# Moving a third token tile's projections from the attention loop into the entry of the linear-attention stage

## The chip, the cores and the metric

The kernel runs on one core of one Trainium2 chip. The metric is device time in microseconds (us) of one execution. The profiled execution gives the trace from which everything below is read; its span starts at its first instruction.

## The reference

Four residual blocks on a sequence of 2048 tokens of width 576, with 32 heads of 18: attention with one shared key/value head (A), then linear attention with Hedgehog features (B), then both again with the same weights.

```python
def A(x, wq, wk, wv, wo):            # one key/value head for 32 query heads
    q = heads(x @ wq); k = x @ wk; v = x @ wv
    p = softmax(einsum("bhqd,bkd->bhqk", q, k) * Dh ** -0.5)
    return merge(einsum("bhqk,bkd->bhqd", p, v)) @ wo
def B(x, wqkv, w_phi, wo):
    q, k, v = split_heads(x @ wqkv)
    phi = lambda t: concat([softmax(t @ w_phi), softmax(-(t @ w_phi))])   # per head
    kv, z = einsum("bhsf,bhsd->bhfd", phi(k), v), phi(k).sum(s)
    return merge(einsum("bhqf,bhfd->bhqd", phi(q), kv) / (phi(q) @ z + 1e-6)) @ wo
for block in (A, B, A, B): x = x + block(layernorm(x))
```

## The kernel before, in words

**Stages.** Tokens are held as 16 tiles of 128. A layer is an A and a B. Per layer there is an attention loop (`attend`) and then a stage that reads the linear attention out and prepares the next layer's queries (in the second layer: writes the output).

**The loop.** 32 groups (16 query tiles by two halves of the heads) run over 16 key tiles and two halves: 1024 units a layer. A unit is two score matmuls on TensorE (PE, L518), one exp of 128x1024 on ScalarE (ACT, L994), and its share of the values matmuls (L806). Results are normalised on VectorE (DVE, L908 to L916), split in high and low parts, and written to DRAM. When both groups of a tile are there, they are read back as `on`.

**What is slipped in.** PE has time beside ACT's exps, and a generator (`stream`, from L1238 on) hands out pieces of other work, a PSUM bank at a time ("fillings", 14 matmuls of 128x288 each, L240): the output projection of a finished tile (weights `wd`, two fillings) and `mix` of a token tile whose residual is done (six fillings: keys `wa`, values `wb`, queries `wc`). In `mix`, `feature_start` (L551 to L558) makes the feature exponents of a half of the heads, `feature_end` (L563 to L565) divides by their sums, `update_state` (L595, 64 small matmuls) adds keys times values to the state `kv` (L601), and the finished query features are turned in blocks of 32 (L647) and spilled to DRAM as `phi`. In the loop DVE does all this; in the stage the products of L565 are on GpSimd (POOL), and features are flipped by PE (L621). In the first layer `fold_phi` (L309 to L364) also runs in the loop: it multiplies `w_phi` into the query and key weights, ten slabs of 288 KB that ACT's queue loads (L332).

**What sets the order.** The order of PE and DVE in the loop is the order in which the code writes the instructions (`in_order` chains them). In the stage a scheduler places them by dependence and priority.

**The entry of the stage.** Tiles 14 and 15 can't be mixed in the loop. `last_mix` (L690) mixes tile 14 beside `last_group` (L858), which normalises the last group: copy of the accumulators (L861), transposes (L864), reciprocals (L868), widening (L870), transposes back (L873), product (L874), split (L133, L134), eight writes and six reads of `on` (L838, L851 to L856). Then come the output projection of tile 15, tile 15's own tokens (`xo`, `xsc`) and mix, the state's transposes (L740), `kvt` (L741), the block matrix `kvb`, and the read-out (L757) and its projection, tile by tile. `prepare` loads `wob` and, in the first layer, `wq` beside it.

Of the kernel before, what the change touches and what calls it, by code (L numbers as in the profile page):

```python
# [61 lines left out]
def kernel(ctx, tc, x_in, wq, wk, wv, wo, wqkv, w_phi, wob, out):  # L62
# [246 lines left out]
    def fold_phi(ps, tmp):  # L309
# [16 lines left out]
        def fetch(n):  # L326
# [3 lines left out]
            st = stage.tile([P, D], F32, name="fstage")  # L330
# [9 lines left out]
        st, following = fetch(0), fetch(1)  # L340
# [3 lines left out]
        short(pl, st)  # L344
        yield -110
        for n, (half, k) in enumerate(units):
            later = fetch(n + 2)
# [15 lines left out]
            short(pl, following)  # L363
            nc.sync.dma_start(scratch[half, k * P : (k + 1) * P, :], fo[:, :D])  # L364
            st, following = following, later
# [240 lines left out]
    def queries(xs, e, st, ps, copies):  # L606
# [3 lines left out]
        if copies is A:  # L610
            for b in range(2):
                feature_end(e, b, G)

# [63 lines left out]
    def mix(i, xs, st, ps, spill, loads, slow, after):  # L677
# [5 lines left out]
        for b in range(2):  # L683
            feature_end(eq, b, V)
        blocks = bw.tile([P, NKG, P], F32, name="pht").rearrange("p a b -> p (a b)")
        spilling = block_transpose(blocks[:, : 2 * D], eq.rearrange("p h s d -> p (h s d)"), spill[i], SPILL)
        next(spilling)
        slow.append(spilling)

    def last_mix(i, stats, st, pool, ps, spill):  # L690
        xn = layer_norm(i, stats, pool, A, "xn" if pool is bw else "xo")
        yield STAGE
        xs = pool.tile([P, 9, P], F32R, name="xs" if pool is bw else "xs3")
        yield from transposed(xn, xs, ps, A, LOE)
        yield STAGE
        if pool is bw:
            ek, eq = (bw.tile([P, H, 2, DH], F32, name=tag) for tag in ("featk", "featq"))
        else:
            both = pool.tile([P, 9, PW], F32, name="xsc").rearrange("p a b -> p (a b)")
            ek, eq = (both[:, k * 2 * D : (k + 1) * 2 * D].rearrange("p (h s d) -> p h s d", s=2, d=DH)  # L700
                      for k in range(2))
        vb = yield from keys_values(i, xs, ek, st, ps, A)
        if pool is bw:
            yield from queries(xs, eq, st, ps, A)
        yield STAGE
        yield from update_state(ek, vb, st, ps)
        st["mixed"] += 1
        yield STAGE
        if pool is not bw:
            yield from queries(xs, eq, st, ps, A)  # L710
            yield STAGE
            yield STAGE
        pht = st["sp"].tile([P, NKG, P], F32, name="phs", bufs=1)
# [14 lines left out]
    def finish_state(st, sp, ps):  # L728
        while st["mixed"] < len(st["left"]):
            yield STAGE  # L730
# [417 lines left out]
    with first, tc.tile_pool(name="ps0", bufs=7, space=PSUM) as ps:  # L1148
# [8 lines left out]
        def advance(job):  # L1157
            while next(job) is not STAGE:
                pass
# [319 lines left out]
```

## Time and profile before

| | us |
|---|---|
| three runs | 2711.14, 2717.02, 2718.07 |
| median | 2717.02 |
| profiled execution | 2717.63 |
| its span | 2715.9 |
| PE busy | 2609.6 (96%) |
| ACT busy | 2149.7 (79%) |
| DVE busy | 1258.2 (46%) |
| first loop, from its first scores | 126.0 to 1248.0 |
| first layer's stage, to its first read-out projection | 1248.0 to 1301.5 |
| second loop's last values end | 2565.0 |
| second stage, to its first read-out projection | 2565.0 to 2618.7 |

A row of the timeline has start and duration, engine, line, operation, output and inputs, how many are merged, and in brackets the idle time of the engine ahead of it with what ended it. A row of windows has the stretch and its length, then busy time (and count) of PE, PE's weight loads, DVE, ACT and POOL, the granted clock of PE as a share of full speed, the DMA engines' busy share and their GB/s.

### The profile page before, as it was taken

To read this page: it belongs to the slowest core of one execution; us is meant where nothing else is said; L and a number is where in the kernel's file an instruction comes from. 1 tells how busy PE (TensorE), PEld (TensorE's weight loads), DVE (VectorE), ACT (ScalarE), POOL (GpSimd) and SP (SyncE) were. 2 spreads that over 40 slices of the span, in tenths; PEclk is the share of its full clock that TensorE was granted. 3 is DMA by queue.
4 is the path that set the end of the run, shared out by engine and by line. 5 is a ranking of instruction groups with operands and counts; after the bars stand their busy time and mean duration, and the time that the engine had idled before them with its cause. 6 is when DMAs were issued, how large, how long until landed. Compare 5 with 4: busy or idle time off the path is not lost. (4 is left out here: it accounts for less than half of the span.)

```text
span 2715.9 us, 55458 instructions
## 1 busy us (share of the span) xinstructions
PE 2609.6 (96%) x22030; PEld 1454.6 (54%) x22030; DVE 1258.2 (46%) x2867; ACT 2149.7 (79%) x2511; POOL 56.8 (2%) x98
## 2 busy tenths in 40 slices
PE   7989999999999999999998999999999999999989
PEld 6633345554555544456997244444444444444588
DVE  8532244445454444445775124444444444444455
ACT  4588898998889879995334999999999999999711
POOL 1000000000000000001000000000000000000010
PEclk9999999999999999999999999999999999999989
DMA  6554134222223212214755412222222222221164
GB/s 192 169 186 140 50 111 130 69 66 58 53 67 72 59 46 57 57 47 112 233 155 161 144 51 59 59 59 59 59 59 59 59 59 59 57 59 48 40 190 144
DMA packets 476349, 245.05 MB, mean 90 GB/s; under 512 B 222706, under 2 KB 433842, under 8 KB 476082
## 3 DMA queue, kind: packets, MB, share of 16 engines
q1 hardware_dynamic: 474610, 238.46, 31.8%
q8 instruction: 177, 2.90, 0.5%
q10 hardware_dynamic: 1472, 2.95, 0.3%
q14 instruction: 90, 0.74, 0.1%
HBM read 133.86 MB, written 105.51 MB: 88 GB/s over the span
## 5 line engine op out<-in xcount | busy, mean ns | idle before, releaser
L994 ACT ACTIVATE pt<-sc 128x1024 f32<-128x1024 f32 x2036 | 1925.4, 1047 | 211.2 <-PE sc L518 191.1
L518 PE MATMUL sc<-qst,kst 56*128 56x512 f32 x3840 | 687.1, 449 | 23.5 <-ACT pt L994 23.0
L518 PEld LDWEIGHTS sc<-qst,kst 56*128 56x128 f32 x3840 | 317.2, 184 | 534.3 <-ACT pt L994 479.4
L806 PE MATMUL acc<-pt,vst 128*32 128x512 f32 x4096 | 499.0, 600 | 0.6 <-DVE featk L551 0.2
L806 PE MATMUL ps<-pt,vst 128*32 128x512 f32 x4048 | 483.5, 601 | 6.5 <-DVE featk L551 6.1
L806 PEld LDWEIGHTS ps<-pt,vst 128*32 128x32 f32 x4048 | 110.1, 109 | 237.4 <-issue 224.2
L806 PEld LDWEIGHTS acc<-pt,vst 128*32 128x32 f32 x4096 | 106.0, 109 | 218.4 <-issue 212.1
L240 PE MATMUL ps<-wahi,xs 128*128 128x288 f32 x792 | 174.5, 306 | 5.7 <-DVE featk L551 3.4
L304 DVE TENSOR_TENSOR xc<-xc,acc 128x288 f32<-128x288 f32 x60 | 27.2, 453 | 321.1 <-PE acc L240 321.1
L240 PEld LDWEIGHTS ps<-wahi,xs 128*128 128x128 f32 x792 | 131.6, 191 | 14.1 <-DVE featk L551 4.2
L240 PE MATMUL ps<-walo,xs 128*128 128x288 f32 x440 | 130.1, 298 | 0.0
L240 PE MATMUL acc<-wdhi,on 128*128 128x288 f32 x540 | 119.7, 307 | 2.0 <-DMA on<-od 2.0
L240 PE MATMUL ps<-wchi,xs 128*128 128x288 f32 x495 | 111.2, 310 | 0.0
L131 ACT ACTIVATE xs<-ps 128x512 fp32r<-128x512 f32 x36 | 21.4, 595 | 112.6 <-PE ps L290 106.3
L396 PE MATMUL ps<-xsc,wbhi 128*128 128x256 f32 x576 | 107.6, 286 | 0.7 <-ACT xsc L131 0.7
L551 DVE COPY featq<-ps 128x288 f32<-128x288 f32 x47 | 21.5, 458 | 179.7 <-PE ps L240 179.6
L418 ACT ACTIVATE pc<-ps 128x256 fp32r<-128x256 f32 x80 | 30.4, 384 | 93.4 <-PE ps L396 90.4
L240 PEld LDWEIGHTS acc<-wdhi,on 128*128 128x128 f32 x540 | 87.9, 187 | 23.9 <-issue 21.1
L396 PEld LDWEIGHTS ps<-xsc,wbhi 128*128 128x128 f32 x576 | 91.4, 193 | 1.6 <-ACT xsc L131 1.1
L240 PEld LDWEIGHTS ps<-wchi,xs 128*128 128x128 f32 x495 | 82.8, 192 | 16.8 <-issue 15.6
L240 PE MATMUL acc<-wdlo,on 128*128 128x288 f32 x300 | 88.2, 294 | 0.0
L396 PE MATMUL ps<-xsc,wblo 128*128 128x256 f32 x320 | 86.1, 284 | 0.0
(260 smaller groups left out, 3066.6 us busy)
## 6 DMA issues: line engine op xcount, KB each, us to landing
qst<-qd SPq DMA_DIRECT2D x360, 72.0 KB
od<-parts SPq DMA_DIRECT2D x512, 36.0 KB
pht<-phi SPq DMA_DIRECT2D x32, 540.0 KB
qd<-pc SPq DMA_DIRECT2D x64, 256.0 KB
phi<-pht SPq DMA_DIRECT2D x112, 144.0 KB
on<-od SPq DMA_DIRECT2D x60, 256.0 KB
xd<-xc SPq DMA_DIRECT2D x32, 288.0 KB
flipped<-pht SPq DMA_DIRECT2D x112, 72.0 KB
```

Source lines behind the costliest of these rows:

```text
L131: A.activation(dst_hi, src, AF.Copy)
L240: T.matmul(dst, xs[:, slot, :], w[half][:, k, c0 : c0 + HALF], start=(n == 0), stop=(n == last))
L304: V.tensor_add(xr, xr, po)
L396: T.matmul(po, lhs, xsc[:, slot, :], start=(n == 0), stop=(n == LASTP))
L418: A.activation(pc[:, 0, :], po, AF.Copy)
L518: T.matmul(sc, kst[head_rows(h), t * P : (t + 1) * P], q[head_rows(h), h // 2, :], start=True, stop=True)
L551: V.tensor_copy(e[:, hs, 0, :], src)
L806: T.matmul(acc[32 * j : 32 * j + 32, :], vst[:, t, :], pts[j], start=first, stop=last)
L994: A.activation(pt, sc, AF.Exp, scale=SCALE)
```

## The change

- Tile 13 (`KEPT`) is not mixed in the loop any more. Its split tokens `xs` are kept; the entry does its keys, values, queries and state. `last_mix` becomes `keys_in` and `queries_in`, and `advance` runs a job to its next finished bank.
- The entry's PE instructions are chained in the order of the code (`add_manual_dep`), from the last values on. `prepare` and `finish_state` stand inline.
- `fold_phi` loads its first three slabs when the loop opens, each later slab one unit ahead, into a pool of the loop.
- In `mix` the first half of the query features is closed within `queries`, and the turning (L647) starts lazily in the queue of slow work.
- The copies at L741 and L861 move from DVE to ACT. `phs` has two buffers, and `xs2` and `featx` are new.

In the loop, PE's order at the second loop's end, before. Names: `sc` scores, `acc` and `ps` PSUM banks, `pt` exps, `wchi`/`wclo` query weights, `osb` the last group's copy.

```order
L240 MATMUL ps<-wclo_18220,xs 128x288
L518 MATMUL sc<-qst,kst 128x512 x6
L806 MATMUL acc<-pt,vst 32x512 x8
L595 MATMUL ps<-featk,vb_17365 32x36 x32
L518 MATMUL sc<-qst,kst 128x512 x6
L806 MATMUL acc<-pt,vst 32x512 x8
L518 MATMUL sc<-qst,kst 128x512 x4
L806 MATMUL acc<-pt,vst 32x512 x4
L518 MATMUL sc<-qst,kst 128x512 x4
L806 MATMUL acc<-pt,vst 32x512 x12
L864 MATMUL ps<-idf,osb 128x128 x4
L290 MATMUL ps<-idf,xn 128x128 x4
```

The same place now:

```order
L518 MATMUL sc<-qst,kst 128x512 x4
L797 MATMUL acc<-pt,vst 32x512 x4
L518 MATMUL sc<-qst,kst 128x512 x2
L797 MATMUL acc<-pt,vst 32x512 x12
L240 MATMUL ps<-wahi,xs 128x288
L240 MATMUL ps<-walo,xs 128x288
L240 MATMUL ps<-wahi,xs 128x288 x2
```

The queries and the update of tile 13 no longer stand among the scores; its keys (`wahi,xs`) are the first work behind the last values.

Later in that entry, PE comes from tile 14's keys (`xs_29367`) to the update of tile 13 (`featk`) and the output projection of tile 15 (`wdhi,on`):

```order
L240 MATMUL ps<-wahi,xs_29367 128x288 x2
L240 MATMUL ps<-walo,xs_29367 128x288
L595 MATMUL ps<-featk,vb_17376 32x36 x32
L240 MATMUL ps<-wdhi,on 128x288
L240 MATMUL ps<-wdlo,on 128x288
```

Before, the output projection stood behind six fillings (all of tile 14) as well; now the six are tile 13's keys and values and tile 14's keys.

DVE at the same entry, before, with the last group's copy and product (`osb`), and its split (`parts`):

```order
L861 COPY osb<-acc 128x512
L868 RECIPROCAL rd<-ps 128x16
L870 COPY wide<-rd 128x512
L134 TENSOR_TENSOR xs<-ps,xs 128x512
L874 TENSOR_TENSOR osb<-osb,ps 128x512
L299 TENSOR_TENSOR xs<-ps,xs 64x128
L133 CAST parts<-osb 128x512
L134 TENSOR_TENSOR parts<-osb,parts 128x512
```

And now:

```order
L553 TENSOR_REDUCE fmax<-ps 128x16
L554 TENSOR_REDUCE fmin<-ps 128x16
L859 RECIPROCAL rd<-ps 128x16
L555 TENSOR_TENSOR featk<-fmin,ps 128x16x18
L861 COPY wide<-rd 128x512
L556 TENSOR_TENSOR featk<-ps,fmax 128x16x18
L865 TENSOR_TENSOR osb<-osb,ps 128x512
L555 TENSOR_TENSOR featk<-fmin,ps 128x16x18
L133 CAST parts<-osb 128x512
L556 TENSOR_TENSOR featk<-ps,fmax 128x16x18
L134 TENSOR_TENSOR parts<-osb,parts 128x512
```

The eight operations that start tile 13's key features (L553 to L556, twice) now stand among the last group's (six of them are in these rows).

DVE in the first loop, where two mixes meet, before:

```order
L134 TENSOR_TENSOR parts<-osb,parts 128x512
L563 TENSOR_REDUCE fz<-featq 128x32
L564 RECIPROCAL fz<-fz 128x32
L565 TENSOR_TENSOR featq<-featq,fz 128x576
L563 TENSOR_REDUCE fz<-featq 128x32
L564 RECIPROCAL fz<-fz 128x32
L565 TENSOR_TENSOR featq<-featq,fz 128x576
L647 STREAM_TRANSPOSE pht<-featq 128x1152
L551 COPY featk<-ps 128x16x18
L553 TENSOR_REDUCE fmax<-featk 128x16
```

And now:

```order
L134 TENSOR_TENSOR parts<-osb,parts 128x512
L563 TENSOR_REDUCE fz<-featq 128x32
L564 RECIPROCAL fz<-fz 128x32
L565 TENSOR_TENSOR featq<-featq,fz 128x576
L551 COPY featk<-ps 128x16x18
L553 TENSOR_REDUCE fmax<-featk 128x16
L554 TENSOR_REDUCE fmin<-featk 128x16
L555 TENSOR_TENSOR featk<-fmin,featk 128x16x18
L556 TENSOR_TENSOR featk<-featk,fmax 128x16x18
L649 STREAM_TRANSPOSE pht<-featq 128x1152
```

Half 0's closing stands further ahead (right behind the exponents of the queries), and the turning has gone behind the copy that empties the next tile's first bank.

The core of the diff:

```diff
@@ fold_phi
-            st = stage.tile([P, D], F32, name="fstage")
+            st = pool.tile([P, D], F32, name="fstage", bufs=3)
...
-        st, following = fetch(0), fetch(1)
+        slabs_in = deque(fetch(n) for n in range(3))
...
-            later = fetch(n + 2)
+            st = slabs_in.popleft()
...
-            short(pl, following)
+            short(pl, slabs_in[0])
+            slabs_in.append(fetch(n + 3))
@@ queries
         if copies is A:
             for b in range(2):
                 feature_end(e, b, G)
+        else:
+            feature_end(e, 0, V)
@@ mix
-        for b in range(2):
-            feature_end(eq, b, V)
...
-        next(spilling)
-        slow.append(spilling)
+        feature_end(eq, 1, V)
+
+        def spilling():
+            blocks = bw.tile([P, NKG, P], F32, name="pht").rearrange("p a b -> p (a b)")
+            yield from block_transpose(blocks[:, : 2 * D], eq.rearrange("p h s d -> p (h s d)"), spill[i], SPILL)
+
+        slow.append(spilling())
@@ stream
-            return (xs is not None and v.left() <= settled
+            return (xs is not None and xs[0] != KEPT and v.left() <= settled
@@ the entry, with the last group's banks
-                for job in (ahead, closing, ahead, closing, ahead, ahead):
-                    advance_to(job)
+                advance(first_keys)
+                next(closing)
+                advance(first_keys)
+                run(closing)
+                advance(first_keys)
+                xs = bw.tile([P, 9, P], F32R, name="xs2")
+                advance(transposed(xn, xs, ps, A, LOE), 2)
+                advance(first_keys)
+                second_keys = keys_in(c - 1, xs, feature_room("featx"), st, ps)
+                advance(second_keys, 2)
+                advance(first_keys)
                 for b in range(2):
                     po = ps.tile([P, HALF], F32, name="ps")
                     run(project(po, st["wo"], b * HALF, on))
                     add_residual(c, b, po)
                 stats = ln_stats([c])
+                advance(second_keys, 2)
@@ the entry, behind it
+                xn = layer_norm(c, stats, sp, A, "xo")
+                advance(second_keys)
+                xl = sp.tile([P, 9, P], F32R, name="xs3")
+                advance(transposed(xn, xl, ps, A, LOE), 2)
...
+                advance(queued[0])
...
+                advance(last_keys, 2)
+                run(load("wob", "a", wob, slice(0, D), engines=(A, V)))
+                advance(last_keys, 2)
...
+                advance(queued[0])
+                advance(last_keys)
+                advance(queued[2])
+                run(finish_state(st, sp, ps))
+                advance(queued[2])
+                advance(queued[1], 2)
...
+                        if before is not None:
+                            tc.add_manual_dep(i, before, NOSYNC, reason="order")
```

Behind it the flips of tiles 13, 14 and 15 (`flips`) and then the read-out of all tiles follow.

More of the change, by code (lines that the diff above doesn't have):

```diff
@@ L682, in mix, with keys_in, queries_in, advance @@
         yield from update_state(ek, vb, st, ps, after=after)
[L683 to L701 removed]
+        feature_end(eq, 1, V)
[3 more added lines that the diff above has]
+        slow.append(spilling())
+    def keys_in(i, xs, ek, st, ps):
         vb = yield from keys_values(i, xs, ek, st, ps, A)
[L703 to L705 removed]
         yield from update_state(ek, vb, st, ps)
[L707 to L713, printed above, removed]
+    def queries_in(i, xs, eq, st, ps, spill):
+        yield from queries(xs, eq, st, ps, A)
+        pht = st["sp"].tile([P, NKG, P], F32, name="phs", bufs=2)
         yield from flip_features(eq, pht, ps, A)
         spill_features(pht, spill, i)
+    def advance(job, count=1):
+        while count:
+            v = next(job, DONE)
+            if v is DONE:
+                return
+            count -= v is not STAGE and not isinstance(v, Kind) and v < 0
     def start_state(bw):
```

66 lines of the change are left out of this document (37 added, 29 removed).

## The prediction

> **What bounds the kernel now.** I read the page's busy times first, then the trace by place, since an average over loops and stages says little.
>
> ```profile
> PE 2609.6 (96%) x22030; PEld 1454.6 (54%) x22030; DVE 1258.2 (46%) x2867; ACT 2149.7 (79%) x2511; POOL 56.8 (2%) x98
> ```
>
> TensorE (PE) is busy 96% of the span, so a gain must take PE work away from where PE is the limit, or fill its waits. The loop has two paces. The timeline of PE in the second loop, where 14 projections (L240) are slipped in:
>
> ```profile
> 2506.32 0.40 PE L240 MATMUL acc<-wahi,xs 128*128 128x288 f32 x1
> ...
> 2508.38 0.97 PE L518 MATMUL sc<-qst,kst 56*128 56x512 f32 x6
> 2509.28 2.78 PE L806 MATMUL ps<-pt,vst 128*32 128x512 f32 x24
> 2511.99 0.97 PE L518 MATMUL sc<-qst,kst 56*128 56x512 f32 x6
> 2512.89 0.40 PE L240 MATMUL acc<-wbhi,xs 128*128 128x288 f32 x1
> ```
>
> Start to start, 2506.32 to 2512.89, is 6.57 us for twelve score matmuls, that is six exps, and one filling. ScalarE (ACT) sets the other pace, in the first loop's tail where nothing is slipped in:
>
> ```profile
> 1229.38 17.52 ACT L994 ACTIVATE pt<-sc 128x1024 f32<-128x1024 f32 x19
> ```
>
> 17.52 / 19 = 0.92 us an exp, 5.53 for six: a filling stretches six exps by 1.04 us. So the loop is held by PE where tiles are mixed and by ACT elsewhere.
>
> **The loops' ends lose tile 13.** These windows (PE, PEld, DVE, ACT and POOL busy) cover both loops from tile 12's state update on; the last row is where the second loop's values end, 2565.02:
>
> ```profile
> 1170.00:1229.00 59.00, 58.46 (x494) 30.60 (x496) 29.29 (x60) 53.81 (x60) 0.54 (x1) 1.00 0.18 44
> 2493.00:2564.00 71.00, 70.45 (x586) 34.16 (x588) 34.48 (x67) 66.36 (x73) 0.54 (x1) 1.00 0.18 43
> ...
> 2561.85 3.17 PE L806 MATMUL acc<-pt,vst 128*32 128x512 f32 x24
> ```
>
> ACT idles 59.00 - 53.81 = 5.2 us in the first, 71.00 - 66.36 = 4.6 in the second, because PE has eight fillings there: six of tile 13 and two output projections of tile 14. The change takes the six, tile 13's update (L595, 0.7 to 0.8 on PE) and its four feature exps on ACT, 2.8 us at the 0.69 to 0.70 that L558 takes here (one L558 row stands with the stall below). If ACT then never waits, the loops end 5.2 + 2.8 = 8.0 and 4.6 + 2.8 = 7.4 us earlier. The two fillings that remain keep at most 2 x 1.04 us; alone among scores, they can be partly taken up by buffered scores, so I take 0.5 off each loop, rounded to -7.4 and -6.9: **-14.3**. Bounds: -5.6 (the eight exps alone) and -15.4.
>
> **The first loop's stalls.** PE's longest waits while tiles are mixed, and VectorE (DVE) and ACT around the longest:
>
> ```profile
> 746.64 0.40 PE L240 MATMUL ps<-wahi,xs 128*128 128x288 f32 x1 [1.68 <-DVE featk L551]
> 808.24 0.41 PE L240 MATMUL ps<-wahi,xs 128*128 128x288 f32 x1 [1.69 <-DVE featk L551]
> 976.09 5.05 PE L806 MATMUL ps<-pt,vst 128*32 128x512 f32 x24 [6.09 <-DVE featk L551]
> ...
> 963.17 0.46 DVE L556 TENSOR_TENSOR featq<-featq,fmax 128x288 f32<-128x288 f32 x1
> 965.07 0.72 DVE L908 STREAM_TRANSPOSE turned<-acc 128x512 f32<-128x512 f32 x1 [1.45 <-PE acc L806]
> ...
> 970.51 0.75 DVE L563 TENSOR_REDUCE fz<-featq 128x32 f32<-128x576 f32 x1
> 972.36 0.74 DVE L563 TENSOR_REDUCE fz<-featq 128x32 f32<-128x576 f32 x1
> 974.32 1.38 DVE L647 STREAM_TRANSPOSE pht<-featq 128x1152 f32<-128x1152 f32 x1
> 975.62 0.42 DVE L551 COPY featk<-ps 128x288 f32<-128x288 f32 x1
> ...
> 977.90 0.68 ACT L558 ACTIVATE featk<-featk 128x576 f32<-128x576 f32 x1 [5.41 <-DVE featk L556]
> ```
>
> PE waits for a PSUM bank that DVE empties with the copy at 975.62, and ACT waits 5.41 as well, so the time is lost. The order now places half 0's closing (970.51 to 972.36, 1.85 us) ahead of L908, where DVE idles 1.45, and the transpose behind the copy (974.32 to 975.62, 1.30 us). The copy comes 1.45 + 1.30 = 2.75 earlier. At 746 and 808 the transpose alone gives 1.30 and the earlier half the rest of 1.68 and 1.69. Sum 2.75 + 1.68 + 1.69 = **-6.1**, bounds 0 (another bank's reader is as late) and -9.5 (all three vanish). The price of moving is that the add of the state (L601) comes up to 1.85 later and the spill of a finished feature block too; PE does not read either before the next tile, so I cost them at nothing, and at a stall of the same 1.7 if that cover fails.
>
> **The stage takes tile 13.** Windows from the last values to the first read-out projection, then that projection's row:
>
> ```profile
> 1248.00:1302.00 54.00, 44.22 (x470) 41.55 (x469) 34.02 (x82) 13.99 (x28) 11.95 (x14) 0.87 0.58 178
> 2565.10:2618.70 53.60, 43.40 (x466) 41.09 (x466) 33.22 (x79) 13.96 (x28) 10.43 (x10) 0.88 0.53 155
> ...
> 2618.67 0.61 PE L240 MATMUL ps<-wahi,xs 128*128 128x288 f32 x1
> ```
>
> Of 53.6 us PE is busy 43.4 and waits 10.2; at a granted clock of 0.88 it loses 0.12 x 53.6 = 6.4 to half clock, so 37.0 us are work at full clock. What it waits for, and the prices of tile 13's work:
>
> ```profile
> 2579.15 0.77 PE L595 MATMUL ps<-featk,vb 128*32 128x36 f32 x64
> 2579.85 0.40 PE L240 MATMUL ps<-wdhi,on 128*128 128x288 f32 x1
> ...
> 2583.52 0.29 PE L240 MATMUL ps<-wdlo,on 128*128 128x288 f32 x1
> 2587.51 0.66 PE L290 MATMUL ps<-idf,xo 128*128 128x128 f32 x4 [3.70 <-ACT xo L280]
> 2588.11 2.29 PE L621 MATMUL ps<-idf,featq 128*108 128x128 f32 x11
> ...
> 2607.39 0.29 PE L240 MATMUL ps<-wclo,xs 128*128 128x288 f32 x1
> 2611.55 0.76 PE L621 MATMUL ps<-idf,xsc 128*108 128x128 f32 x5 [2.06 <-POOL xsc L565]
> 2613.64 1.53 PE L621 MATMUL ps<-idf,xsc 128*108 128x128 f32 x6 [1.33 <-POOL xsc L565]
> ```
>
> 28 projections take 2583.81 - 2579.85 = 3.96, at full clock about 3.8, so 14 take 1.9. Tile 13 brings 6 x 1.9 + 0.7 + 1.2 (eleven flips, half of 2.29, a row at half clock) = 13.3: work 50.3. The 3.70 wait goes: tile 15's tokens are now made while the values projection of tile 14 runs. What is late next is the other end. Tile 14's query projections now come last, and their features go through DVE, ACT and POOL before PE can flip them. Before, the same chain of tile 15 kept PE's flips from 2607.68, where its last projection ends, to 2611.55 (3.9, with a read-out inside) and for 1.33 more. Now tile 13's flips (1.2) are all that lies inside: 2.7 + 1.3 = 4.0. Then the heads of the last group, `on`:
>
> ```profile
> 2569.77 0.69 DVE L134 TENSOR_TENSOR parts<-osb,parts 128x512 fp32r<-128x512 f32 x1
> ...
> 2577.38 0.45 SPq L856 DMA_DIRECT2D on<-od x1
> ```
>
> The parts are done at 2570.46, 5.4 after the loop; the reads back are issued by 2577.83, and their first user at 2579.85 (14.8 after the loop) did not wait. Now that user stands behind six fillings, the transposes and one update, at 6 x 1.9 + 1.2 + 0.7 = 13.3, and the parts stand on DVE behind eight more feature operations (L553 to L556, 0.46 as in the row above, started every 0.4), of which some fall in DVE's own waits: an estimated 2.5 us. The wait is 0 to 14.8 + 2.5 - 13.3 = 4.0; I take 1.5, since the landing may well be earlier than 14.8. Everything behind it on PE waits too, since PE's order there is fixed. One more wait on POOL, somewhat under the 1.33: 1.1. Together 6.6.
>
> Half clock follows waits:
>
> ```profile
> 2598.63:2602.04 3.41, 1.75 (x71) 1.44 (x72) 0.80 (x3) 0.36 (x1) 1.17 (x2) 1.00 0.91 302
> 2602.04:2605.45 3.41, 3.41 (x17) 3.35 (x15) 1.34 (x2) 0.00 (x0) 0.00 (x0) 0.50 0.87 318
> ```
>
> A stretch of 3.41 us with PE busy 1.75 is followed by one at 0.50. I count one such stretch near the end, 1.7. [...]
>
> The stage becomes 50.3 + 6.6 + 1.7 = 58.6, **+5.0 in each layer, +10.0**. Bounds: +0.7 (50.3 + 4.0, all else hidden) and +9.2 (`on` at 4.0, a second and half a third stretch of half clock). Copies moved from DVE to ACT cost 0.6 to 0.7 on either; weight slabs loaded earlier are split on engines with ACT busy 14 of 53.6: nothing, within these bounds.
>
> **The slabs.** Three of 288 KB leave the start:
>
> ```profile
> 0.76 1.37 ACTq L332 DMA_DIRECT2D fstage<-in_B_wqkv_dram  x3
> 4.98 0.82 DVE L266 BATCH_NORM_STATS2 bnst<-xall 128x6 f32<-128x288 f32 x2 [1.56 <-DMA xall<-in_A_x_dram]
> ...
> 4.00:6.00 2.00, 0.00 (x0) 0.00 (x0) 1.01 (x3) 0.00 (x0) 0.00 (x0) 1.00 1.05 408
> 126.00:150.00 24.00, 23.14 (x162) 7.38 (x166) 6.46 (x20) 23.08 (x26) 0.00 (x0) 1.00 0.42 145
> ...
> L332 ACTq DMA_DIRECT2D fstage<-in_B_wqkv_dram x12: 334/428/609, 0.8 to 283.1; - x12
> ```
>
> With DMA at its limit (408 GB/s), the slab bytes ahead of the first tokens cost about 0.7 us (some 0.3 MB); bounds 0 and 2.1 (all 864 KB). Their three issues, 0.43 each, now stand in ACT's queue at the loop's head, where ACT is busy 23.08 of 24: +1.3, bounds 0 and 1.8. Later slabs are issued behind the same exps as before: no change. Net **+0.6**.
>
> **The sum.** The profiled execution took 2717.6 us, the span 2715.9 and 1.7 around it; the median of three runs, 2717.0, lies 0.6 below, so I keep its scale: 2717.6 - 14.3 - 6.1 + 10.0 + 0.6 = **2707.8**.
>
> **Rivals.**
> - *The stage hides tile 13.* Its 13.3 us meet 10.2 of waits and 6.4 of half clock. For it: both are as large as the work. Against it: the feature chain at the end. At +0.7 each: 2707.8 - 2 x 4.3 = 2699.2.
> - *The stalls stay.* Another tile's row on DVE holds the bank: 2713.9. Against it: the order moves exactly the instructions ahead of the copy.
> - *The loop does not shorten*, as ACT finds other waits: 5.6 instead of 14.3, 2716.5. Against it: 17.52 for 19.
> - *Slower:* `on` comes late. The round trip from 2570.46 to at most 2579.85 is 9.4; if the SP queue, with the tile's other transfers in it, makes it twice that, PE stands 9.4 longer with nothing to pass it, and one more half-clock stretch: 11.1 each, 2730.0. It decides from 9.8 / 2 = 4.9 per stage on. For it: PE's fixed order, and a chain of eight writes and six reads through DRAM. Against it: before, the same chain was through without a wait on PE.
> [...]
>
> **How the numbers follow.** Forecast 0.44; stage hides it 0.18; stalls stay 0.17; slower 0.10; loop does not shorten 0.06; lenient clock 0.05. The range, 2698 to 2720, takes in all but the late `on` and the outer part of the first rival. A change of 0.3% (8.2 us, so 2708.9 and 2725.2) is about what a measurement of this kernel can tell from none. Below 2708.9 lie the hidden stage, the lenient clock and six tenths of the forecast, with a little of the rest: faster 0.52. Slower holds most of the late `on`: 0.08. Same 0.40.
>
> **What would show it.** In the changed profile: no 6.09 wait at L797, but some 3.3; ACT dense at 0.92 an exp after tile 12's update; a wait on DMA at the first matmul on `on` of 0 to 4; waits for POOL's L565 ahead of tile 14's flips; first read-out projection some 58.6 after the last values. I am wrong if the stage grows by 10, or if PE's waits in the first loop have only moved.

## The result, and the profile after

Eleven runs of the changed kernel took 2709.95 us in the median (2706.75 to 2712.62), eleven of the kernel before 2714.41 (2711.14 to 2718.83). The ratio is 0.9976, with a 95% interval of 0.9968 to 0.9984: faster by 0.24%, some 6.5 us (the two medians alone differ by 4.5). The profiled executions lie 7.7 us apart (spans 2708.2 and 2715.9). Line numbers of the changed kernel: L985 is the exp, L797 the values, L748 the read-out, L623 the flips, L899 the transposition of a finished group.

The first row of its page: PE has gained share, since what it waits for went while its work did not.

```profile
PE 2616.8 (97%) x22052; PEld 1447.8 (53%) x22052; DVE 1236.9 (46%) x2839; ACT 2154.5 (80%) x2529; POOL 65.9 (2%) x106
```

I cut both executions at the same events of PE's timeline (start of the loop's first scores behind the branch, start of a state update in the loop, end of the last values, start of the second read-out projection of tile 0's and 1's rows) and took differences. The nine stretches add up to the spans. Each kernel was profiled once, so a difference of a microsecond or two in one row can be scatter: to the second loop's tile 12, twelve kernels took 1183.4 to 1186.7 us with no order by the change, and the -1.15 there is not put down to it.

| stretch, us | before | after | difference | forecast |
|---|---|---|---|---|
| start to the first loop's first scores | 126.01 | 124.14 | -1.87 | -0.7 |
| to tile 0's update (weights folded here) | 320.37 | 322.73 | +2.36 | +1.3 |
| to tile 12's update | 722.85 | 720.34 | -2.51 | -6.1 |
| to the loop's last values | 78.79 | 72.08 | -6.71 | -7.4 |
| to the second read-out projection | 59.40 | 64.53 | +5.13 | +5.0 |
| to the second loop's tile 12 | 1184.71 | 1183.56 | -1.15 | 0 |
| to its last values | 72.89 | 66.57 | -6.32 | -6.9 |
| to the second read-out projection | 61.24 | 64.36 | +3.12 | +5.0 |
| to the end | 89.64 | 89.89 | +0.25 | 0 |

**The loop's end.** ACT's timeline in the second loop, from tile 12's update on:

```profile
2488.67 20.27 ACT L985 ACTIVATE pt<-sc 128x1024 f32<-128x1024 f32 x22 [0.86 <-PE sc L518]
2509.12 5.79 ACT L985 ACTIVATE pt<-sc 128x1024 f32<-128x1024 f32 x6 [0.19 <-PE sc L518]
2515.78 5.80 ACT L985 ACTIVATE pt<-sc 128x1024 f32<-128x1024 f32 x6 [0.86 <-PE sc L518]
...
2522.52 30.33 ACT L985 ACTIVATE pt<-sc 128x1024 f32<-128x1024 f32 x33
```

30.33 / 33 = 0.92 us an exp: ACT is dense, as forecast. The two fillings that stayed (tile 14's output projection, at 2509 and 2516) still make it wait about 1 us between them and the row ahead 0.86 more; I had allowed 0.5 for both.

**The stage.** PE's timeline of the second entry, in its order: the heads' first user, the last flips with their waits, and the first read-out projection. Then the stage's window and that of its last 14 us.

```profile
2567.39 0.40 PE L240 MATMUL ps<-wdhi,on 128*128 128x288 f32 x1
...
2601.83 0.76 PE L623 MATMUL ps<-idf,featq 128*108 128x128 f32 x5 [2.67 <-POOL featq L565]
2604.07 1.53 PE L623 MATMUL ps<-idf,featq 128*108 128x128 f32 x6 [1.48 <-POOL featq L565]
...
2610.06 0.69 PE L290 MATMUL ps<-idf,xo 128*128 128x128 f32 x4 [1.02 <-DVE den L756]
...
2612.43 0.40 PE L240 MATMUL ps<-wahi,xs 128*128 128x288 f32 x1
```

```profile
2554.00:2612.40 58.40, 52.69 (x624) 50.37 (x624) 40.69 (x100) 19.95 (x41) 14.98 (x14) 0.97 0.45 135
2598.00:2612.00 14.00, 8.84 (x115) 7.56 (x115) 7.63 (x20) 6.75 (x16) 4.57 (x4) 0.88 0.44 126
```

From 2553.95, where the values end, to 2612.43 it is 58.5 us (58.6 in the first layer), and 58.6 was forecast. PE waits 58.40 - 52.69 = 5.7 us in it, against 10.2 before: tile 13's work stands where PE waited for tile 15's tokens (the 3.70 of before is 0.5 now), and the chain of tile 14's query features has become the end, 2.67 + 1.48 = 4.2. `on` is there without a wait. Half clock costs (1 - 0.88) x 14 = 1.7 us, all of it at this end. Before, it took 0.12 x 53.6 = 6.4 of the stage. So of tile 13's work, 50.9 - 37.0 = 13.9 us at full clock, 4.5 went where waits had been and 4.7 where half clock had been, and the remaining 4.7 made the stage longer. PE's longest wait in this stage is the 2.67 us that ends at 2601.83, and the one stretch at half clock, 3.41 us long, begins at 2603.75.

**The first loop's waits.** PE, and DVE ahead of two of them:

```profile
508.45 1.92 PE L797 MATMUL acc<-pt,vst 128*32 128x512 f32 x16 [0.87 <-DVE kv L601]
613.90 0.77 PE L595 MATMUL acc<-featk,vb 128*32 128x36 f32 x64 [1.15 <-DVE turned L899]
974.67 1.93 PE L797 MATMUL ps<-pt,vst 128*32 128x512 f32 x12 [2.86 <-DVE featk L551]
```

```profile
506.67 0.76 DVE L565 TENSOR_TENSOR featq<-featq,fz 128x576 f32<-128x576 f32 x1
507.35 0.71 DVE L899 STREAM_TRANSPOSE turned<-ps 128x512 f32<-128x512 f32 x1
507.98 0.42 DVE L601 TENSOR_TENSOR kv<-kv,acc 128x288 f32<-128x288 f32 x1
...
612.47 0.76 DVE L565 TENSOR_TENSOR featq<-featq,fz 128x576 f32<-128x576 f32 x1
613.14 0.71 DVE L899 STREAM_TRANSPOSE turned<-acc 128x512 f32<-128x512 f32 x1
```

The 6.09 of before is 2.86, and 1.68 and 1.69 are gone. But half 0's closing (its last step at 506.67 and 612.47) now stands ahead of the two jobs that empty a PSUM bank for PE, L899 and L601, and PE waits for them at 508 and 614.

**The start.** DVE's first tokens, PE's first transposes and the loop's first scores:

```profile
3.79 0.82 DVE L266 BATCH_NORM_STATS2 bnst<-xall 128x6 f32<-128x288 f32 x2 [0.38 <-DMA xall<-in_A_x_dram]
...
8.13 1.12 PE L290 MATMUL ps<-idf,xn 128*128 128x128 f32 x4 [8.13 <-ACT xn L280]
...
124.14 1.14 PE L518 MATMUL sc<-wclo,kst 56*128 56x512 f32 x6 [0.70 <-ACTq L1008]
```

Tokens are there 1.2 us earlier (4.98 before), and the loop opens 1.87 earlier.

### The profile page after: what moved, and what is told of

It is laid out like the page before. It is cut to its first block, busy times and chain, and to the rows that moved or that the text cites. A ratio compares the mean times of both kernels' runs of the same rounds, so it can differ in the third digit from the quotient of the medians.

```text
span 2708.2 us, 55518 instructions
## 1 busy us (share of the span) xinstructions
PE 2616.8 (97%) x22052; PEld 1447.8 (53%) x22052; DVE 1236.9 (46%) x2839; ACT 2154.5 (80%) x2529; POOL 65.9 (2%) x106
## 5 line engine op out<-in xcount | busy, mean ns | idle before, releaser
L985 ACT ACTIVATE pt<-sc 128x1024 f32<-128x1024 f32 x2036 | 1922.7, 1055 | 206.9 <-PE sc L518 187.2
L518 PE MATMUL sc<-qst,kst 56*128 56x512 f32 x3840 | 699.0, 452 | 26.4 <-ACT pt L985 26.0
L797 PE MATMUL acc<-pt,vst 128*32 128x512 f32 x4096 | 502.6, 602 | 1.5 <-DVE kv L601 0.9
L797 PE MATMUL ps<-pt,vst 128*32 128x512 f32 x4048 | 485.1, 601 | 3.3 <-DVE featk L551 2.9
L797 PEld LDWEIGHTS ps<-pt,vst 128*32 128x32 f32 x4048 | 109.1, 109 | 229.9 <-issue 223.0
L797 PEld LDWEIGHTS acc<-pt,vst 128*32 128x32 f32 x4096 | 104.5, 109 | 213.3 <-issue 207.5
L240 PEld LDWEIGHTS acc<-wdhi,on 128*128 128x128 f32 x540 | 87.9, 187 | 23.5 <-issue 20.6
L551 DVE COPY featq<-ps 128x288 f32<-128x288 f32 x44 | 20.1, 457 | 170.2 <-PE ps L240 170.0
L271 POOL TENSOR_TENSOR rstd<-var,neghalf 128x1 f32<-128x1 f32 (+1 forms) x56 | 32.0, 571 | 2400.0 <-DVE var L269 2377.9
```

Source lines behind the costliest of these rows:

```text
L240: T.matmul(dst, xs[:, slot, :], w[half][:, k, c0 : c0 + HALF], start=(n == 0), stop=(n == last))
L271: G.tensor_tensor(rstd, var, neghalf[:, :n], op=ALU.pow)
L518: T.matmul(sc, kst[head_rows(h), t * P : (t + 1) * P], q[head_rows(h), h // 2, :], start=True, stop=True)
L551: V.tensor_copy(e[:, hs, 0, :], src)
L797: T.matmul(acc[32 * j : 32 * j + 32, :], vst[:, t, :], pts[j], start=first, stop=last)
L985: A.activation(pt, sc, AF.Exp, scale=SCALE)
```

## The experiments

My theory behind the result: the slabs give 1.9 us at the start; the features' closing gives some 2.5, because what it takes from one bank's wait it gives back to two others; tile 13's move gives the rest; and the fold's stretch takes 2.4 back by chance of the clock. The rivals are named with each run. Each kernel's one profile is cut like the table above; the profiled executions of e4 and e6 were the slowest of their runs. `opens` is the loop's opening, `fold` from there to tile 0's update, `mixes` to tile 12's, `end+stage` from tile 12's update to the second read-out projection, in each layer:

| kernel | slabs moved | closing | tile 13 | opens | fold | mixes | end+stage 1 | end+stage 2 |
|---|---|---|---|---|---|---|---|---|
| before | no | as before | loop | 126.01 | 320.37 | 722.85 | 138.19 | 134.13 |
| e1 | yes | as before | loop | 123.34 | 324.10 | 723.25 | 136.59 | 134.10 |
| e2 | no | in two | loop | 125.35 | 320.13 | 720.32 | 137.29 | 131.78 |
| changed | yes | in two | entry | 124.14 | 322.73 | 720.34 | 136.61 | 130.93 |
| e3 | yes | as before | entry | 123.57 | 319.74 | 723.05 | 136.62 | 131.69 |
| e4 | yes | turning late | entry | 124.25 | 325.57 | 721.34 | 136.52 | 131.48 |
| e5 | yes | all late | entry | 123.62 | 320.97 | 713.20 | 136.92 | 131.72 |
| e6 | yes | in two | entry, flips 13, 15, 14 | 124.14 | 323.97 | 720.08 | 137.75 | 130.24 |
| e7 | yes | in two | entry, `on` early | 123.80 | 325.09 | 720.33 | 143.40 | 138.73 |
| e8 | yes | in two | entry, no chain | 123.57 | 323.47 | 720.16 | 136.06 | 130.60 |
| e9 | yes | all late | entry, half 1 on DVE | 124.02 | 320.97 | 713.88 | 136.37 | 130.09 |
| e10 | yes | all late | loop | 123.99 | 320.85 | 713.06 | 137.49 | 132.54 |

### e1: the slabs alone

```diff
-            st = stage.tile([P, D], F32, name="fstage")
+            st = pool.tile([P, D], F32, name="fstage", bufs=3)
...
-        st, following = fetch(0), fetch(1)
+        slabs_in = deque(fetch(n) for n in range(3))
```

> The kernel before with the three slabs of fold_phi moved from the start to the loop's opening, and nothing else. Theory one (the slabs only compete for DMA with the first tokens): the loop's first scores behind the branch start 1.9 us earlier than the 126.01 of before, the stretch from there to the first slab's transpose stays at 26.4 us, and everything behind is as before except for half-clock stretches in the fold phase (150 to 330 us) that come and go by chance, 0 to 3 us; time 0 to 2 us below before. Rival (the slab issues on ACT's queue cost what they take, 1.3 us, and the half-clock stretches of the changed kernel in 190 to 268 us are made by them): the stretch grows by 1.3 us, the two half-clock stretches are there again, and the time is the same as before or up to 1 us above.

Measured: 2715.39 us, ratio 0.9993 (0.9983 to 1.0004). The loop opened 2.67 us earlier, and from there to the first slab's transpose it took 26.45, as before (26.44): the issues on ACT's queue cost nothing, which speaks against the rival. The fold's stretch was longer by 3.7. Half clock stands behind a wait near 191 us again, as in the changed kernel, but not at 248; it comes at 273 and 331 instead, so only one of the rival's two stretches is back:

```profile
170.00:193.00 23.00, 19.96 (x125) 7.14 (x123) 11.85 (x22) 16.92 (x18) 0.00 (x0) 0.87 0.50 154
193.00:215.00 22.00, 21.68 (x157) 11.14 (x161) 2.80 (x6) 19.04 (x21) 0.00 (x0) 0.97 0.83 279
248.40:267.50 19.10, 17.54 (x127) 6.75 (x123) 5.34 (x11) 16.65 (x18) 0.00 (x0) 1.00 0.24 71
```

So some 2 us are won at the start (e2, with the slabs where they were, opened 0.7 earlier than before, so 2.67 has scatter in it) and can be lost in the fold; the time alone can't tell this from no change.

### e2: the features closed in two, alone

```diff
+        else:
+            feature_end(e, 0, V)
...
-        for b in range(2):
-            feature_end(eq, b, V)
...
-        next(spilling)
-        slow.append(spilling)
+        feature_end(eq, 1, V)
...
+        slow.append(spilling())
```

> The kernel before with the query features closed in two and the turning started late, and nothing else. My theory: PE's wait at the values block near 976 falls from 6.09 to 2.9 us, the waits at 746 and 808 (1.68, 1.69) vanish but give only 0.5 us each, and the earlier closing of half 0 costs some 2.3 us between the first and the fourth state update, in waits for the adding of the state (0.9) and for the last group's first transposition on DVE (1.2); in all the first loop ends 2.5 us earlier. The second loop does not change. Time 2 to 3 us below before. Rival (the losses between the first updates are chance, as the clock is): the first loop ends 5 us earlier or more.

Measured: 2712.19 us, ratio 0.9994 (0.9984 to 1.0004), not told from no change by time. The trace tells it: `mixes` is 720.32, 2.53 less than before and equal to the changed kernel (720.34), with the same waits:

```profile
507.29 1.93 PE L809 MATMUL acc<-pt,vst 128*32 128x512 f32 x16 [0.84 <-DVE kv L601]
...
612.74 0.77 PE L595 MATMUL acc<-featk,vb 128*32 128x36 f32 x64 [1.14 <-DVE turned L911]
...
973.47 4.24 PE L809 MATMUL ps<-pt,vst 128*32 128x512 f32 x24 [2.86 <-DVE featk L551]
```

The losses are not chance: they come again to 0.03 us.

### e3: the changed kernel, features closed as before

```diff
-        else:
-            feature_end(e, 0, V)
...
-        feature_end(eq, 1, V)
+        for b in range(2):
+            feature_end(eq, b, V)
...
+        next(spilling)
+        slow.append(spilling)
```

> The changed kernel with the features closed as before (both halves behind the update, turning at once), so tile 13's move and the slabs alone. My theory: the waits of 1.68, 1.69 and 6.09 us are back, the two of 0.9 and 1.2 us are gone, so that the first loop up to tile 12's update is 2.5 us longer than in the changed kernel; both stages and both loops' ends as in the changed kernel (stage 58.6 and 58.5 us, loop's end 72.1 and 66.6). Time some 2.5 us above the changed kernel, 4 to 5 below before. Rival (closing in two is what makes room at the loops' ends): the loops' ends come out longer by more than 1 us.

Measured: 2711.87 us, ratio 0.9989 (0.9979 to 0.9998). `mixes` is 723.05, 2.7 more than in the changed kernel, and the old waits are back:

```profile
743.59 0.40 PE L240 MATMUL ps<-wahi,xs 128*128 128x288 f32 x1 [1.70 <-DVE featk L551]
...
805.19 0.40 PE L240 MATMUL ps<-wahi,xs 128*128 128x288 f32 x1 [1.70 <-DVE featk L551]
...
972.88 5.35 PE L794 MATMUL ps<-pt,vst 128*32 128x512 f32 x24 [6.09 <-DVE featk L551]
```

The loops' ends with the stages are within 0.8 us of the changed kernel, so the closing is not what makes room there. The loops' ends alone, 72.09 and 66.59 us, are those of the changed kernel (72.08 and 66.57), so this rival fell.

### e4: only the turning late

```diff
-        else:
-            feature_end(e, 0, V)
...
-        feature_end(eq, 1, V)
+        for b in range(2):
+            feature_end(eq, b, V)
```

> The changed kernel with only the turning left late: both halves of the query features are closed behind the update. My theory: the early half is what brings the two new waits (0.9 us for the adding of the state, 1.2 us for DVE's transposition of a finished group), so both go and the first loop gains some 2 us before the fourth update; near 976 the wait is 6.09 - 1.30 = 4.8 us instead of 2.9, a loss of 1.9. In all within 1 us of the changed kernel. Rival (the two waits come from the late turning): they stay, and the kernel is 1.5 to 2 us slower than the changed one.

Measured: 2709.92 us, ratio 0.9978 (0.9969 to 0.9988), as the changed kernel. The waits at 508 and 614 are gone, so it is the early half that makes them. Near 976:

```profile
977.99 5.09 PE L796 MATMUL ps<-pt,vst 128*32 128x512 f32 x24 [4.70 <-DVE featk L551]
```

4.70 where 6.09 - 1.30 = 4.8 was expected: the wait is as long as DVE's queue ahead of the copy. `mixes` came to 721.34. Up to the fourth update the gain was 1.0 us and not 2: the first two updates lie 1.0 us further apart than in the changed kernel. Between them PE waits 0.4 us for ACT and 0.5 for a DMA in e4; why is open.

### e5: both halves closed late

```diff
-        else:
-            feature_end(e, 0, V)
...
-        feature_end(eq, 1, V)
 
         def spilling():
+            for b in range(2):
+                feature_end(eq, b, V)
+                yield
```

> The changed kernel with both halves of the query features closed late, as the first two steps of the slow work that then turns them, behind the copy that empties the next tile's first bank. My theory (what PE waits for near 976 is only the length of DVE's queue ahead of that copy; the early half is what made the waits of 0.9 and 1.2): the copy comes 2 x 1.85 + 1.30 = 5.0 us earlier than in the kernel before, so the wait of 6.09 (2.86 in the changed kernel) falls to 1.1 or less, the two waits of 0.9 and 1.2 between the first and the fourth update are gone, and the first loop from its first update to tile 12's takes 715 to 717 us instead of 720.3; time 3 to 5 us below the changed kernel. Rival (another of DVE's jobs is as late, or the later turning holds up the next tile's spill): a new wait on DVE of 1 us or more somewhere among the mixes, and the time within 1 us of the changed kernel.

Measured: 2702.03 us (2701.04 to 2703.44), ratio 0.9948 (0.9935 to 0.996), the fastest here beside e9, and 7.9 us below the changed kernel's median (7.6 by the ratios to the kernel before, each taken beside its own runs). PE's longest wait on DVE among the mixes:

```profile
965.59 2.78 PE L797 MATMUL ps<-pt,vst 128*32 128x512 f32 x24 [1.00 <-DVE featk L551]
```

1.00 was expected as 1.1. `mixes` is 713.20, 7.1 below the changed kernel, where I had expected 3 to 5. Cut at each state update, e5 gains on the kernel before 6.0 us between tile 9's and tile 10's (the long wait) and 1.65 and 1.68 at the two places of the short ones (tile 5's to 6's, 6's to 7's), and within 0.65 everywhere else. The changed kernel gains 3.5, 0.46 and 0.48 there. So the short waits are worth all of their 1.7 once both halves are out of the way. ACT in the changed kernel at the first of these places, DVE ahead of it, and ACT in e5:

```profile
744.43 1.93 ACT L985 ACTIVATE pt<-sc 128x1024 f32<-128x1024 f32 x2
747.76 0.69 ACT L558 ACTIVATE featk<-featk 128x576 f32<-128x576 f32 x1 [1.40 <-DVE featk L556]
```

```profile
743.60 0.75 DVE L563 TENSOR_REDUCE fz<-featq 128x32 f32<-128x576 f32 x1
744.38 0.35 DVE L564 RECIPROCAL fz<-fz 128x32 f32<-128x32 f32 x1
744.77 0.76 DVE L565 TENSOR_TENSOR featq<-featq,fz 128x576 f32<-128x576 f32 x1
745.44 0.45 DVE L551 COPY featk<-ps 128x288 f32<-128x288 f32 x1
```

```profile
739.53 2.86 ACT L985 ACTIVATE pt<-sc 128x1024 f32<-128x1024 f32 x3 [0.61 <-PE sc L518]
742.26 0.69 ACT L558 ACTIVATE featk<-featk 128x576 f32<-128x576 f32 x1
```

In the changed kernel PE no longer waits for the bank there, but half 1's closing still stands ahead of the next key features on DVE (L551). ACT, whose queue has their exp (L558) ahead of further exps, waits 1.40 for them, and PE then waits for ACT's exps (0.24 and 0.41 at 750.33 and 751.24). In e5 DVE starts the key features at 739.62, and neither PE nor ACT waits for DVE.

### e6: the last flips in the order 13, 15, 14

```diff
-                return queued
+                return [queued[0], queued[2], queued[1]]
```

> The changed kernel with the order of the last flips 13, 15, 14 instead of 13, 14, 15. My theory (the chain of tile 14's query features through DVE, ACT and POOL ends last, while tile 15's features are long done): tile 15's eleven flips, 1.2 to 1.3 us at full clock, fill the first of the two waits of 2.67 and 1.48 us, so 2.67 falls to about 1.4 and each stage is 1.2 to 2.5 us shorter (the latter where a half-clock stretch goes as well); time 2.5 to 5 us below the changed kernel. Rival (ACT's copies of the flipped blocks set the end): the second wait grows by what the first loses, and the stages stay within 0.5 us of 58.6 and 58.5.

Measured: 2708.15 us, ratio 0.997 (0.9958 to 0.9982); end and stage together +1.1 in the first layer, -0.7 in the second. My theory fell:

```profile
2605.21 0.87 PE L623 MATMUL ps<-idf,xsc 128*108 128x128 f32 x6 [2.17 <-POOL xsc L565]
2607.38 2.65 PE L623 MATMUL ps<-idf,featq 128*108 128x128 f32 x11 [1.30 <-POOL featq L565]
```

Tile 15's features are not long done; they pass through the same DVE and POOL. The waits of 2.67 and 1.48 became 2.17 and 1.30; the second stage, with the same granted clock of 0.97, is shorter by just that, and the first, which is longer, had a clock of 0.91. The rival named another cause (ACT's copies), for which nothing speaks either: the rows name POOL.

### e7: the heads wanted 4.5 us earlier

```diff
                 second_keys = keys_in(c - 1, xs, feature_room("featx"), st, ps)
-                advance(second_keys, 2)
-                advance(first_keys)
                 for b in range(2):
                     po = ps.tile([P, HALF], F32, name="ps")
                     run(project(po, st["wo"], b * HALF, on))
                     add_residual(c, b, po)
                 stats = ln_stats([c])
+                advance(second_keys, 2)
+                advance(first_keys)
                 advance(second_keys, 2)
```

> The changed kernel with the output projection of tile 15 ahead of tile 14's keys and tile 13's update, so that PE wants the heads read back (on) 4.5 us earlier, some 9 us behind the last values. It measures when they land. My theory after the result: their last piece lands just in time in the changed kernel (its issue ends 13.5 us behind the last values, PE wants the first piece at 13.4), so PE now waits for DMA about 4 us, and the stage is up to 4 us longer. Rival (they land long before): a wait under 1 us, and the heads' way through DRAM had several us to spare, so that it could never have made the change slower.

Measured: 2728.09 us, one run, the profiled one. In the second layer the values ended at 2564.33, and

```profile
2576.53 0.37 PE L240 MATMUL ps<-wdhi,on 128*128 128x288 f32 x1 [2.33 <-DMA on<-od]
...
2578.46 1.14 PE L240 MATMUL ps<-wdhi,on 128*128 128x288 f32 x2 [0.61 <-DMA on<-od]
```

PE waited 2.33 + 0.61 = 2.9 us (1.76 + 1.61 = 3.4 in the first layer). The first six matmuls on `on` ran ahead of these reads, so they use pieces read back before; the seventh needs the first new piece and the twelfth the last. They came 12.2 and 14.1 us behind the last values (11.6 and 14.9 in the first layer). In the changed kernel the same two stand at 14.3 and 15.0, so at most about 1 us is to spare for the last piece, as the theory had it, though the first piece has 2. But the price was larger than I expected: end and stage grew by 6.8 and 7.8 us. Beside the waits it is half clock: over the two stages the granted clock was 0.92 and 0.90 against 0.97, which is 3.5 and 4.9 us, and in the 15 us behind the second layer's waits it was 0.83:

```profile
2580.00:2595.00 15.00, 14.41 (x206) 13.76 (x205) 8.27 (x21) 3.48 (x7) 3.50 (x4) 0.83 0.49 158
```

### e8: PE's order not fixed

```diff
-                before = None
-                for i in traced(nc)[mark:]:
-                    if i.engine == mybir.EngineType.PE:
-                        if before is not None:
-                            tc.add_manual_dep(i, before, NOSYNC, reason="order")
-                        before = i.name
```

> The changed kernel without the chain that fixes PE's order in the entry; the scheduler places PE's instructions there. It moves only the transposes of the last group (a few projections earlier) and pieces of tile 15's tokens. My theory (the scheduler finds nearly the same order, so the chain is worth little): both stages within 1 us of 58.6 and 58.5, time within 1.5 us of the changed kernel. Rival (the chain is what keeps the way to the heads or the feature chain short): a stage longer by 2 us or more.

Measured: 2709.06 us, ratio 0.9971 (0.9959 to 0.9982). End and stage are 0.55 and 0.33 us shorter than with the chain. The chain is worth nothing here, and costs nothing that can be told.

### e9: the second half's product on DVE

```diff
-            for b in range(2):
-                feature_end(e, b, G)
+            for b, engine in enumerate((G, V)):
+                feature_end(e, b, engine)
```

(on e5)

> The kernel with both halves closed late (as before this run), and in the entry the second half of every tile's query features multiplied on DVE instead of POOL. My theory (the end of the entry is a chain through DVE and POOL, in which the second half's product of 1.17 us on POOL stands behind the first's): DVE does it in 0.76 and beside POOL, so the second wait for POOL among the flips, 1.21 to 1.48 us, falls under 0.4, and each stage is about 1 us shorter; time 1 to 3 us below the kernel with both halves closed late (2702). Rival (DVE is the longer queue there): the first wait, 2.67, grows by as much, and the stages stay within 0.5 us, clock aside.

Measured: 2702.53 us, ratio 0.9947 (0.9934 to 0.9961), like e5. The flips' waits in the second layer:

```profile
2595.67 1.31 PE L621 MATMUL ps<-idf,featq 128*108 128x128 f32 x5 [3.04 <-POOL featq L565]
2597.29 1.50 PE L621 MATMUL ps<-idf,featq 128*108 128x128 f32 x6 [0.31 <-DVE featq L565]
```

The second wait fell to 0.31 (0.86 in the first layer), the first rose by 0.37: both theories hold in part, and end and stage are 0.55 and 1.6 us shorter than in e5, where half clock held for one stretch of 3.41 us more. Time does not show it.

### e10: tile 13 back in the loop, all else kept

```diff
-        for b in range(2):
-            feature_end(eq, b, V)
...
-        next(spilling)
-        slow.append(spilling)
+            for b in range(2):
+                feature_end(eq, b, V)
+                yield
...
+        slow.append(spilling())
```

(on e1, that is the kernel before with the slabs moved)

> The kernel before with the slabs moved and both halves closed late, tile 13 mixed in the loop as before: what the move of tile 13 itself is worth beside the others. My theory (the loops' ends win 6.5 us each, the stages lose 4 to 5 each): from tile 12's update to the second read-out projection it takes 136.6 to 138.2 us in the first layer and 131.7 to 134.1 in the second, against 136.6 and 131 with the move; so the time lies 1 to 5 us above the kernel with the move (2702). Rival (the move is worth nothing, all of the gain is the features' closing and the slabs): within 1 us of it.

Measured: 2704.07 us, ratio 0.9953 (0.9939 to 0.9966), 2.0 above e5's median (1.4 by the ratios). The intervals overlap, so the time doesn't settle it. The table helps: the four kernels with tile 13 in the loop have 137.4 and 133.1 us for end and stage in the mean, the four with an unaltered new entry (changed, e3, e4, e5) 136.7 and 131.5. The move is worth about 0.7 + 1.7 = 2.4 us in these means. Three pairs differ in these stretches by the move alone: e1 to e3 wins 0.0 + 2.4 us, e10 to e5 0.6 + 0.8, e2 to changed 0.7 + 0.9. So it is 1.4 to 2.4 us, and only the traces show it: e3's runs lie 3.5 us below e1's in the median and 1.6 in the mean, with a scatter of 2.3 on that. The copies moved to ACT belong to what is called the move here; they were not tried alone. By far the largest single step of all runs is the late closing: 722.85 to 713.

## Why the prediction was right, point by point

The measured 2709.95 lies 2.1 us above the predicted 2707.8 and well within the range; the direction was right. That it is so close is in part luck. The forecast was a gain of 9.8 us; the profiles show 7.7, the ratio 6.5 and the medians 4.5; the kernel before came out 2.6 us lower in eleven runs than in the three that the sum started from. And errors of the terms offset each other: the stalls gave 3.6 less than forecast, the second stage cost 1.9 less, the start and the second loop gave 1.2 and 1.15 more. By the bound of 0.3% that I had set, 0.24% is "same" (0.40), not "faster" (0.52).

- **The loops' ends** (-14.3): -6.7 and -6.3, -13.0. Right mechanism; the two remaining fillings keep 1.1 to 1.3 us of the 2.1 that they could, where I had 0.5. (8.0 - 0.5 is 7.5 and not the 7.4 of the sum, a slip of 0.1.)
- **The stages** (+10.0): +5.1 and +4.8 up to the first read-out projection, where I had cut. Work 50.3 against 52.69 - 0.03 x 58.4 = 50.9, waits 6.6 against 5.7 (4.2 at the flips, where I had 4.0; `on` 0 where I had 1.5; and in place of the further wait on POOL of 1.1, 1.0 for DVE's `den` and 0.5 for tile 15's tokens), half clock 1.7 against 1.7. For `on` I had taken the wrong user: the first six matmuls on it don't need the last group. The upper bound is added wrongly: its terms give +10.1 and not +9.2. The cut hid one thing: in the second layer of before, the first read-out itself ran largely at half clock (granted clock 0.74 from 2618.67 to 2626.20; 7.6 us to the next instead of 5.9), and this went; so the stage lost only 3.1 by the second projection. And the +5 rests on the half clock of before, which is not fixed: e2, with tile 13 in the loop, had its first stage in 49.7 us at a granted clock of 0.97, where before took 53.5 at 0.87. Against that stage the move would have cost 9.
- **The stalls** (-6.1): the sum's weakest term. The waits themselves moved as worked out (2.86 for 6.09 - 2.75 = 3.34, none at 746 and 808). Two steps failed. The one that costed the later adding of the state "at nothing, and at a stall of the same 1.7 if that cover fails": the cover failed, with 0.87 us for the adding, and 1.15 more came at the transposition of a finished group (L899), which I had not named; e2 and e4 show that it is the early half. And the two short waits gave back only about 0.5 us each: the wait of PE for the bank became one of ACT (1.40) for the key features, which still stood behind half 1's closing on DVE; e5, without it, gets the full 1.65 and 1.68. From tile 3's update (485 us into the loop) to tile 12's the changed kernel won 4.8; up to there from tile 0's it lost 2.3. So the sign that I had set for being wrong, that PE's waits have only moved, is there in part.
- **The slabs** (+0.6): mis-sized on both sides. The start gave 1.9 (in the bound of 2.1), since the weights behind the tokens come earlier too (ACT starts on `wq` at 5.62 instead of 8.08); the issues on ACT's queue cost 0 and not 1.3, in ten kernels alike (26.4 us from the loop's opening to the first slab).
- **What was not in the sum**: the fold's stretch, +2.4, is half clock: it held for 17.1 us there against 10.2 before, 3.4 us of time, and without it the stretch would be 1.0 shorter. e3, with the slabs moved, has 319.74, less than before; and changed, e6, e7 and e8, which run the same instructions up to there, have 322.73 to 325.09. An effect of the change on how often half clock comes is not shown, and not excluded.
- **The rivals**: that the stages hide tile 13 fell; the late `on` did not come, but e7 shows that its margin was at most about 1 us and its price some 7 us a stage, so 0.10 was not too much. The lenient clock (0.05), a stage without half clock, is shown by no run: the granted clock was 0.87 and 0.88 in the stages before and 0.97 in both of the changed kernel, with half clock for 3.41 us of each.

## What to carry to other kernels

What the buffer's reader waited for here was the engine's queue ahead of the one job that frees the buffer (6.09 us before, 4.70 with the turning behind that job, 2.86 with one closing out of the way as well, 1.00 with both): move the other jobs behind it, all of them, and look at which jobs the moved ones now stand ahead of (0.87 and 1.15 us of new waits here). Work moved from a place where it costs its full time into a stage full of waits can cost less than its time (here 13.9 us of work made the second stage 4.7 us longer), but the stage's new end can then be the chain that starts last (4.2 us of waits here), and has to be walked by hand. Where a sum is cut at an event, see that the clock is the same on both sides of the cut (here the stretch behind it took 7.6 us, at a granted clock of 0.74, and then 5.9 at 1.00).

## What the runs showed of the hardware that I had not expected

Half clock comes and goes in nearly the same instructions. From the loop's opening to tile 0's update twelve kernels took 319.7 to 325.6 us; the spread of 5.8 us is nearly that of the whole change. Half clock held for 10.2 to 20.5 us of it, and with half of that taken off all twelve lie between 314.0 and 315.6. The windows of the changed kernel and of before at the same two places of the fold:

```profile
190.80:214.00 23.20, 22.92 (x157) 11.18 (x157) 2.81 (x6) 18.49 (x21) 0.00 (x0) 0.93 0.79 259
247.60:268.20 20.60, 19.18 (x123) 7.18 (x123) 5.39 (x11) 16.73 (x19) 0.00 (x0) 0.92 0.23 66
```

```profile
193.00:215.00 22.00, 21.67 (x158) 10.85 (x158) 2.80 (x6) 18.72 (x21) 0.00 (x0) 1.00 0.85 277
248.40:267.50 19.10, 17.57 (x123) 6.75 (x123) 5.39 (x10) 16.64 (x19) 0.00 (x0) 1.00 0.25 71
```

0.07 x 23.2 + 0.08 x 20.6 = 3.3 us of clock, with the same waits ahead of both. The traces also show what differs. In the kernel before and in the changed one the time between two changes of the granted clock is a whole number of steps of 3.4133 us, to within 0.01 us. Near 190 us both have the same wait of PE, 1.80 us. In the changed kernel 1.57 of it fall into one such step, and half clock follows; in the kernel before it is split over two, 1.09 and 0.71, and none does:

```profile
187.12:190.53 3.41, 1.85 (x16) 0.78 (x8) 3.24 (x7) 3.21 (x4) 0.00 (x0) 1.00 0.00 0
190.53:193.94 3.41, 3.17 (x13) 1.17 (x15) 0.47 (x3) 0.61 (x2) 0.00 (x0) 0.50 0.39 91
```

```profile
188.82:192.23 3.41, 2.32 (x20) 0.91 (x12) 2.98 (x6) 3.23 (x5) 0.00 (x0) 1.00 0.00 0
192.23:195.64 3.41, 2.69 (x19) 1.17 (x19) 0.95 (x3) 1.89 (x3) 0.00 (x0) 1.00 0.33 78
```

PE was busy 1.85 us of the step ahead of the half clock, and 2.32 and 2.69 of the steps of before. The busy share of a step alone does not decide: at 248.55 us of the changed kernel half clock followed one with PE busy 2.46, with the clock full till then. What decides is not shown.
